# Attention and a hidden layer on one core: masks built in steps, exp(h) kept in PSUM, a low-bit step on ScalarE, the range check last

## The chip, the cores and the metric

The kernel runs on one core of a Trainium2 chip. A core has a matrix engine (TensorE, PE in the profile), three engines for elementwise work (VectorE = DVE, ScalarE = ACT, GpSimd = POOL) and SyncE (SP), which here issues the DMA transfers. Each engine takes its own instructions in order and waits on semaphores for the others. The metric is the device time of one execution in microseconds (us); smaller is better.

## The reference

The input holds 4 sequences of 768 tokens and 8 heads of 64. Each token attends to itself and the 127 before it, and to the first `n_sink` = 4 tokens of its sequence. The result goes through a layer of 2048 hidden units with an ELU.

```python
scores = scale * np.matmul(q, k.transpose(0, 1, 3, 2))
keep = is_sink | in_window
scores = np.where(keep, scores, -1000000000.0)
...
a = a / (np.sum(a, axis=-1, keepdims=True) + 1e-09)
return np.matmul(a, v).astype(np.float32)
...
h = x @ w_in
g = np.where(h > 0.0, h, alpha * (np.exp(np.minimum(h, 0.0)) - 1.0))
return (g @ w_out).astype(np.float32)
```

Here x is the attention's result, 3072 tokens of 512. The hidden layer's weights (512 x 2048 and 2048 x 512) arrive as float64; q, k and v are float32.

## The kernel before

**Precision.** Products are made of 16-bit halves. An operand is split into a rounded high half (by ScalarE) and the rest (by VectorE or GpSimd), and TensorE adds three products: high·high, high·low, low·high.

**Chunks.** The 24 tiles of 128 tokens are cut into nine chunks (`SIZES`): three of two tiles (256 tokens), then six of three (384). For each chunk, attention gives `x` (four pairs of heads), then the hidden layer runs over 16 groups `f` of 128 hidden units. The first two chunks are done in halves (`PARTS`): groups 0 to 7 of chunk 0, the same of chunk 1, then groups 8 to 15 of both.

**Weights** (`weights`, `weight_f32`). 32 pieces of 128 x 512, two for each group (the even piece is of `w_in`, the odd one of `w_out`), are loaded once, in the first part of the run (the ramp), in which the attention of the first chunks runs as well. A piece is 128 x 1024 words of float64 halves in `raw`. Four steps make a float32 of it: ScalarE scales the upper words into a PSUM bank, `acc[2]` (L267); VectorE shifts out the three bits that the lower word adds (L268, 16-bit integers) and takes the sign bit (L269), both into `wu`; VectorE joins the three (L270). Then ScalarE makes the high half (L416) and GpSimd the low one (L417). There are two buffers `wu` and six `raw`.

**Attention.** TensorE makes scores (L540, L541; L547 in the first two chunks), VectorE adds the mask and takes the row's minimum of the negative in one instruction (L566), ScalarE takes exp and its sum (L568), then the probabilities are split (L580 on ScalarE, L581 on VectorE) and a DMA transposes them from `pq` to `pt` (L599). TensorE multiplies with V into the single bank `po` (L610), and ScalarE and VectorE copy it out as the two halves of `x` (L623, L624); the next pair needs `po` after that.

**Hidden layer.** TensorE adds 12 products into a bank of `h` (L651). ScalarE takes exp into `g` in SBUF (L659), VectorE makes `(e - 1) * scale` in place (L661) and joins it with `h` (L662), ScalarE and GpSimd split it (L664, L665), and two groups later TensorE adds it to the chunk's output banks `acc` (L672). At the end ScalarE and VectorE copy `acc` out (L695, L697), and SP stores it.

**Masks.** `make_masks` makes three masks from `n_sink` and `window`: `m0` for a sequence's first tile, `m1` for its second, `m2` for the others. `attention_moe` first reads the two integers, makes floats of them (L940 to L945) and checks their range (L948 to L952).

**Range check.** The fast path is valid for bounded values. `in_range` (L723) reduces the sums collected on the way on VectorE, a tiny matmul (L741) spreads the verdict over the partitions, and `decide` (L733) writes the flag, which each engine reads at the end to branch past `general_path`.

**Order.** The order on every engine comes from `Plan`: each step is a task with an engine, an estimated length and dependencies. TensorE's order is written down by positions (`pos`); the others are listed by a greedy schedule with due times from TensorE's. So an estimate changes the order on ScalarE, VectorE, GpSimd and SP.

Of the kernel before, what the change touches and what calls it, by code (L numbers as in the profile page):

```python
# [280 lines left out]
def make_masks(nc, tmp, sk, nw, m0, m1, m2):  # L281
# [13 lines left out]


    nc.vector.tensor_scalar(own, rel, nw[:, 1:2], None, ALU.is_lt)
    nc.vector.tensor_scalar(kp, rel, 0.0, None, ALU.is_ge)
    nc.vector.tensor_tensor(own, own, kp, ALU.mult)

    nc.vector.tensor_copy(kp, own)
# [11 lines left out]
    nc.gpsimd.memset(m1[:, 0:NS], MASKED)

    def rest():
        to_mask(m2[:, KW + NS : 2 * KW], own)
        nc.vector.tensor_copy(kp[:, 0:NS], rel[:, 0:NS])
        to_mask(m2[:, NS:KW], kp)
        to_mask(m2[:, 0:NS], sk)

    return rest


def fast_path(tc, ctx, first, kq, vx, wt, out, nw, flag):
# [672 lines left out]
```

## Time and profile before

| | |
|---|---|
| median of 3 runs | 664.21 us (663.05 to 664.29) |
| the profiled execution | 662.14 us, its span 660.3 us |
| mean granted clock of TensorE | 0.984 |
| busy: TensorE, its weight loads | 609.9 us, 370.2 us |
| busy: VectorE, ScalarE, GpSimd | 458.4 us, 456.9 us, 338.2 us |
| transfers | 93.41 MB, 141 GB/s on average |

The span runs from the first to the last instruction; the execution's time has 1.84 us around it. The busy tenths of the page show three parts, 16.5 us to a digit:

```
PE   3486799789999999999999999999999999999996
DVE  6999998896677776667677776758677787524222
ACT  4999786777788887767677777766677777523221
```

TensorE reaches nine tenths after about a quarter of the span and keeps it to the last slice. How to read the rows that follow: a row of a group has the line, engine, operation, output and inputs with their shapes, the count, busy us and mean ns, then the idle time in front and who ended it. A row of a timeline starts with the start and length in us.

### The profile page before, as it was taken

The numbers are of one execution on the slowest core, as the hardware profiler recorded it, in microseconds if no ns is written. First come the engines' busy times: TensorE is split into PE (matmuls) and PEld (weight loads), VectorE is DVE, ScalarE is ACT, GpSimd is POOL, SyncE is SP. The second block draws the span as 40 slices with busy tenths as digits, with TensorE's granted clock in tenths as the row PEclk, the third lists the DMA queues.
The fourth block names the chain that finished last, engine by engine and source line by source line (L and its number), as shares of the span: only waits on it lengthen the run. The fifth ranks groups of instructions, "written<-read, shape, count | busy, mean of one in ns | idle before, by whom it ended". The sixth has DMA issues, their size and how long they took to land.

```text
span 660.3 us, 13443 instructions
## 1 busy us (share of the span) xinstructions
PE 609.9 (92%) x4449; PEld 370.2 (56%) x4449; DVE 458.4 (69%) x1251; ACT 456.9 (69%) x1340; POOL 338.2 (51%) x497
## 2 busy tenths in 40 slices
PE   3486799789999999999999999999999999999996
PEld 2343466456776665555555556555555565555552
DVE  6999998896677776667677776758677787524222
ACT  4999786777788887767677777766677777523221
POOL 0158866785556666544555655444446564322221
PEclk9999698899999999999999999999999999999998
DMA  7989974857654586435454566555554734211001
GB/s 264 206 282 266 276 199 144 269 142 167 145 118 128 136 184 131 116 92 171 116 152 118 133 156 167 104 111 171 112 155 128 208 84 101 49 56 49 1 0 54
DMA packets 130110, 93.41 MB, mean 141 GB/s; under 512 B 104432, under 2 KB 109552, under 8 KB 130032
## 3 DMA queue, kind: packets, MB, share of 16 engines
q1 hardware_dynamic: 130032, 92.47, 53.2%
q8 instruction: 37, 0.61, 0.4%
q14 instruction: 41, 0.34, 0.2%
HBM read 59.94 MB, written 7.34 MB: 102 GB/s over the span
## 4 chain that ended last, share of the span: by engine, by line
PE 78%; DVE 7%; ACT 5%; issue 4%; POOL 3%; DMA 3%; SPq 0%; DVEq 0%; POOLq 0%; ACTq 0%
PE h L651 33%; PE acc L672 33%; PE po L610 5%; PE s L540 3%; PE s L541 3%; DMA pt<-pq 2%; PE s L547 1%; ACT e L568 1%; DVE wu L268 1%; POOL kq L487 1%; DVE wv L270 1%; DVE wu L269 1%; DVE pq L581 1%; DVE g L661 1%; POOL kq L489 1%
## 5 line engine op out<-in xcount | busy, mean ns | idle before, releaser
L651 PE MATMUL h<-x,w 128*128 128x384 f16 (+1 forms) x1728 | 276.6, 310 | 5.6 <-DVE g L662 5.6
L665 POOL TENSOR_TENSOR gl<-g,gh 128x384 f16<-128x384 f32 (+1 forms) x144 | 126.9, 882 | 215.2 <-ACT gh L664 184.4
L651 PEld LDWEIGHTS <-w 128*128 128x128 f16 x1728 | 165.6, 99 | 98.7 <-issue 5.9
L672 PE MATMUL acc<-w,gh 128*128 128x512 f16 x768 | 195.3, 384 | 0.8 <-DVE wv L693 0.8
L661 DVE TENSOR_SCALAR g<-g 128x384 f32<-128x384 f32 (+1 forms) x144 | 65.3, 454 | 115.8 <-ACT g L659 115.3
L659 ACT ACTIVATE g<-h 128x384 f32<-128x384 f32 (+1 forms) x144 | 64.9, 451 | 88.3 <-PE h L651 83.1
L581 DVE SCALAR_TENSOR_TENSOR pq<-e,st,pq 128x256 f16<-128x256 f32 (+1 forms) x192 | 107.2, 587 | 19.7 <-ACT pq L580 19.1
L672 PE MATMUL acc<-w,gl 128*128 128x512 f16 x384 | 110.6, 383 | 0.6 <-POOL gl L665 0.4
L672 PEld LDWEIGHTS <-gh 128*128 128x128 f16 x768 | 70.9, 98 | 71.5 <-issue 3.0
L568 ACT ACTIVATE e<-e,st 128x264 f32<-128x264 f32 (+1 forms) x192 | 93.4, 487 | 11.1 <-DVE st L566 9.7
L664 ACT ACTIVATE gh<-g 128x384 f16<-128x384 f32 (+1 forms) x144 | 69.3, 481 | 44.6 <-DVE g L662 44.2
L566 DVE CUSTOM_DVE_ANT_0 e<-s,m 128x264 f32<-128x264 f32 (+1 forms) x192 | 73.0, 404 | 32.1 <-PE s L541 26.8
L580 ACT ACTIVATE pq<-e,st 128x256 f16<-128x256 f32 (+1 forms) x192 | 85.1, 480 | 10.5 <-DVE st L573 10.1
L487 POOL TENSOR_TENSOR kq<-kqs,kq 128x396 fp32r<-128x396 f32 (+1 forms) x56 | 67.2, 1199 | 23.9 <-ACT kq L483 23.0
L662 DVE SCALAR_TENSOR_TENSOR g<-g,h 128x384 f32<-128x384 f32 (+1 forms) x144 | 72.6, 504 | 1.6
L672 PEld LDWEIGHTS <-gl 128*128 128x128 f16 x384 | 37.6, 99 | 47.9 <-POOL gl L665 2.5
L483 ACT ACTIVATE kq<-kqs 128x780 fp32r<-128x780 f32 (+2 forms) x56 | 48.4, 879 | 17.1 <-PE s L541 14.3
L417 POOL TENSOR_TENSOR w<-wv,w 128x512 f16<-128x512 f32 x32 | 39.5, 1236 | 38.8 <-ACT w L416 18.9
L489 POOL TENSOR_TENSOR kq<-kqs,kq 64x384 fp32r<-64x384 f32 (+1 forms) x56 | 56.7, 1013 | 4.4
L610 PE MATMUL po<-pt,vh 128*64 128x128 f16 x704 | 41.7, 230 | 17.8 <-DMA pt<-pq 7.8
L540 PE MATMUL s<-kq 128*128 128x264 f32 x160 | 56.2, 370 | 1.7 <-POOL kq L489 1.6
L610 PEld LDWEIGHTS <-vh 128*64 128x64 f16 x704 | 31.1, 115 | 29.6 <-issue 21.7
(78 smaller groups left out, 629.2 us busy)
## 6 DMA issues: line engine op xcount, KB each, us to landing
raw<-in_wt_dram SPq DMA_DIRECT2D x32, 512.0 KB, 5.6
kqs<-in_kq_dram SPq DMA_DIRECT2D x24, 456.0 KB, 3.4
kqs<-in_kq_dram SPq DMA_DIRECT2D x24, 390.0 KB, 3.3
out_dram<-wv SPq DMA_DIRECT2D x24, 256.0 KB, 2.5
vs<-in_vx_dram SPq DMA_DIRECT2D x20, 256.0 KB, 3.1
vm<-in_vx_dram SPq DMA_DIRECT2D x6, 768.0 KB, 4.6
kqs<-in_kq_dram SPq DMA_DIRECT2D x12, 326.0 KB, 4.1
vs<-in_vx_dram SPq DMA_DIRECT2D x12, 320.0 KB, 3.1
```

Of the source, the lines that this page charges most:

```text
L487: nc.gpsimd.tensor_tensor(buf[:, KQ_MAX : KQ_MAX + n] if c >= DUP else buf[:, kw : 2 * kw], raw[:, :n], hi[:, :n].bitcast(F32), ALU.subtract)
L540: nc.tensor.matmul(sp[:, :wd], q, hi[:, c0 : c0 + wd], start=True, stop=False)
L566: red = add("DVE", 0.13 + 0.00145 * wd, lambda ee=ee, me=me, sp=sps[e], m=m, wd=wd: nc.vector.tensor_tensor_reduce(ee, sp[:, :wd], m[:, :w ...
L568: ex = add("ACT", 0.48 + 0.00085 * wd, lambda ee=ee, me=me, rs=rs[:, e : e + 1]: nc.scalar.activation(ee, ee, AF.Exp, bias=me, scale=-1.0, ...
L580: a = add("ACT", act_us(nb * P, True), lambda src=src, hi=hi, re=re: nc.scalar.activation(hi, src, AF.Copy, scale=re), deps=[rr])
L581: b = add("DVE", dve_us(nb * P) + 0.1, lambda src=src, hi=hi, lo=lo, re=re: nc.vector.scalar_tensor_tensor(lo, src, re, hi, ALU.mult, ALU. ...
L610: nc.tensor.matmul(po[e * D : (e + 1) * D, oc], vv[:, vo : vo + D], pt[:, (2 * e + part) * nb + i, :], start=new, stop=last)
L651: nc.tensor.matmul(hp[:, :n], win[:, part, d, :], xx[:, :n], start=k == 0, stop=k == 3 * ND - 1)
L661: b = add("DVE", 0.1 + 0.0008 * n, lambda gf=gf: nc.vector.tensor_scalar(gf, gf, -1.0, G_SCALE, ALU.add, ALU.mult), deps=[a])
L662: b = add("DVE", dve_us(n), lambda gf=gf, hp=hp: nc.vector.scalar_tensor_tensor(gf, gf, 0.0, hp[:, :n], ALU.min, ALU.max), deps=[b])
L665: tl = add("POOL", pool_us(n), lambda gl=gl, gf=gf, gh=gh: nc.gpsimd.tensor_tensor(gl[:, :n], gf, gh[:, :n], ALU.subtract), deps=[th])
L672: nc.tensor.matmul(acc[i], gg[:, i * P : (i + 1) * P], wout[:, part, :], start=f == f0 and k == 0, stop=f == f1 - 1 and k == 2)
```

## The change

Four edits, and the planner's estimates with them.

1. The masks are made by a generator in four steps. Before the integers are there: what needs only the row numbers, and the constant columns (GpSimd). Then `m0`, then `m1`, then `m2`; the last two are tasks of the plan, on which the first reductions of a second and a third tile depend. `m0` and `m1` write the four sink columns again in place of a copy. The range check of the integers (`allowed`) becomes a task of its own, wanted by the last check only.
2. Where exp(h) fits beside h in its PSUM bank (256 tokens: chunks 0 to 2), ScalarE writes it there and L661's successor (L673) reads it from there.
3. For every even piece of weights (`ON_ACT`) the shift by 13 bits is an activation of ScalarE (L276): multiply by 2^-13, add a little less than -1/2, round to a 16-bit integer.
4. The range check waits for the last group's `g`, and its matmul stands behind all others.

```diff
+ON_ACT = range(0, NW, 2)
...
+    if on_act:
+        steps[1] = lambda: nc.scalar.activation(ui[:, :, 0], halves[:, :, 1], AF.Copy, scale=2.0**-13, bias=-4095.5 / 8192)
+    return steps
...
+    nc.vector.tensor_scalar(kp, rel, 0.0, None, ALU.is_ge)
...
+    yield
+
+    nc.vector.tensor_scalar(sk, sk, nw[:, 0:1], None, ALU.is_lt)
+    nc.vector.scalar_tensor_tensor(own, rel, nw[:, 1:2], kp, ALU.is_lt, ALU.mult)
+    to_mask(m0[:, NS:KW], own)
+    nc.vector.tensor_tensor(kp[:, 0:NS], own[:, 0:NS], sk, ALU.max)
+    to_mask(m0[:, NS : 2 * NS], kp[:, 0:NS])
+    yield
     to_mask(m1[:, KW + NS : 2 * KW], own)
     nc.vector.tensor_scalar(kp, rel, float(P), nw[:, 1:2], ALU.add, ALU.is_lt)
-    nc.vector.tensor_copy(rel[:, 0:NS], kp[:, 0:NS])
-    nc.vector.tensor_tensor(kp[:, 0:NS], kp[:, 0:NS], sk, ALU.max)
     to_mask(m1[:, NS:KW], kp)
+    nc.vector.tensor_tensor(rel[:, 0:NS], kp[:, 0:NS], sk, ALU.max)
+    to_mask(m1[:, NS : 2 * NS], rel[:, 0:NS])
+    yield
+    to_mask(m2[:, KW + NS : 2 * KW], own)
+    to_mask(m2[:, NS:KW], kp)
+    to_mask(m2[:, 0:NS], sk)
+    yield
...
-    rest_ = add("DVE", 0.9, rest)
+    mask1 = add("DVE", 1.0, lambda: next(masks))
+    mask2 = add("DVE", 0.6, lambda: next(masks), deps=[mask1])
+    allowed = add("DVE", 0.7, allowed)
...
-            u1 = add("DVE", 0.65, step(1), deps=[ld])
+            u1 = add("ACT", act_us(512), step(1), deps=[ld]) if k in ON_ACT else add("DVE", 0.65, step(1), deps=[ld])
...
-        tl = add("POOL", 1.5, ...
+        tl = add("POOL", 1.22, ...
...
-            a = add("ACT", act_us(n) + 0.06, lambda gf=gf, hp=hp, sums=sums: nc.scalar.activation(gf, hp[:, :n], AF.Exp, scale=1.0 / G_SCALE, accum_out=sums), deps=[s1])
+            ex = hp[:, n : 2 * n] if 2 * n <= 512 else gf
+            a = add("ACT", act_us(n) + 0.15, lambda ex=ex, hp=hp, sums=sums: nc.scalar.activation(ex, hp[:, :n], AF.Exp, scale=1.0 / G_SCALE, accum_out=sums), deps=[s1])
-            b = add("DVE", 0.1 + 0.0008 * n, lambda gf=gf: nc.vector.tensor_scalar(gf, gf, -1.0, G_SCALE, ALU.add, ALU.mult), deps=[a])
+            b = add("DVE", 0.4 if 2 * n <= 512 else 0.45, lambda gf=gf, ex=ex: nc.vector.tensor_scalar(gf, ex, -1.0, G_SCALE, ALU.add, ALU.mult), deps=[a])
...
-    a = add("DVE", 2.0, in_range, deps=seen + exps_done)
-    b = add("PE", 0.1, lambda: nc.tensor.matmul(sp[:, 0:3], ones, some16, start=True, stop=True), deps=[a], pos=start + 2 * LAG - 1.5)
+    a = add("DVE", 2.0, in_range, deps=seen + exps_done + g_done[-1:] + [allowed])
+    b = add("PE", 0.1, lambda: nc.tensor.matmul(sp[:, 0:3], ones, some16, start=True, stop=True), deps=[a], pos=start + 2 * LAG)
```

Three places of the order show what moves. First VectorE's, near its beginning. Before the change, the last rows ahead of the first reduction of scores (L566); the range check of the integers (L948 to L951) and five more rows stand ahead of these.

```order
L294 TENSOR_SCALAR m1_173<-pt5_108 128x128
L294 TENSOR_SCALAR m2_174<-pt5_108 128x128
L302 TENSOR_TENSOR pt5_108<-pt5_108 128x4
L294 TENSOR_SCALAR m0_172<-pt5_108 128x128
L309 TENSOR_SCALAR pt5_108<-pt5_108,words_58 128x128
L310 COPY pt5_108<-pt5_108 128x4
L311 TENSOR_TENSOR pt5_108<-pt5_108 128x4
L294 TENSOR_SCALAR m1_173<-pt5_108 128x128
L317 COPY pt5_108<-pt5_108 128x4
L294 TENSOR_SCALAR m2_174<-pt5_108 128x128
L294 TENSOR_SCALAR m2_174<-pt5_108 128x4
L566 ISA e0_91,st0_94<-s0_166,m0_172 128x132
```

In the changed kernel all that stands there behind the integers' conversion:

```order
L307 TENSOR_SCALAR pt5_99<-pt5_99,words_58 128x4
L309 SCALAR_TENSOR_TENSOR pt5_99<-pt5_99,words_58 128x128
L303 TENSOR_SCALAR m0_163<-pt5_99 128x128
L312 TENSOR_TENSOR pt5_99<-pt5_99 128x4
L303 TENSOR_SCALAR m1_164<-pt5_99 128x128
L303 TENSOR_SCALAR m0_163<-pt5_99 128x4
L317 TENSOR_SCALAR pt5_99<-pt5_99,words_58 128x128
L303 TENSOR_SCALAR m1_164<-pt5_99 128x128
L319 TENSOR_TENSOR pt5_99<-pt5_99 128x4
L303 TENSOR_SCALAR m1_164<-pt5_99 128x4
L576 ISA e0_82,st0_85<-s0_157,m0_163 128x132
L576 ISA st0_85 128x1
```

Of 20 instructions behind the conversion ten are left ahead of the first reduction; the writes of `m2` stand behind the two reductions of the first tile, the integers' range check 28 rows behind the first of them.

Second, ScalarE's order where chunk 0's attention ends: the second to the fourth copy of `x` out of `po`, with the weight steps between (`acc2` is the scaled upper words, `w` a finished high half). Before:

```order
L623 ACTIVATE x_117<-po0_168 128x256
L510 ACTIVATE vh1_87<-vs1_73 128x384
L267 ACTIVATE acc2_171<-raw2_128 128x512
L416 ACTIVATE w1_133<-wv1_121 128x512
L623 ACTIVATE x_117<-po0_168 128x256
L510 ACTIVATE vh0_86<-vs0_72 128x512
L267 ACTIVATE acc2_171<-raw3_129 128x512
L416 ACTIVATE w2_134<-wv2_122 128x512
L267 ACTIVATE acc2_171<-raw4_130 128x512
L416 ACTIVATE w3_135<-wv3_123 128x512
L623 ACTIVATE x_117<-po0_168 128x256
```

And after the change:

```order
L633 ACTIVATE x_108<-po0_159 128x256
L520 ACTIVATE vh1_78<-vs1_64 128x384
L426 ACTIVATE w0_123<-wv0_111 128x512
L270 ACTIVATE acc2_162<-raw2_119 128x512
L633 ACTIVATE x_108<-po0_159 128x256
L276 ACTIVATE wu0_115<-raw2_119 128x512
L426 ACTIVATE w1_124<-wv1_112 128x512
L270 ACTIVATE acc2_162<-raw3_120 128x512
L426 ACTIVATE w2_125<-wv2_113 128x512
L633 ACTIVATE x_108<-po0_159 128x256
L270 ACTIVATE acc2_162<-raw4_121 128x512
L276 ACTIVATE wu0_115<-raw4_121 128x512
```

The copies keep their rows; two rows that make low bits (`wu0`) stand behind the third and the fourth copy, and each finished weight comes one piece later.

Third, VectorE's order at the end of the run: `g` of the last group, the check (`checks`, `some`), the flag in `words`, and the last copies out of `acc`. Before:

```order
L727 TENSOR_REDUCE some_203<-checks_202 128x1 x2
L728 TENSOR_SCALAR checks_202<-checks_202 128x32
L729 TENSOR_REDUCE some_203<-checks_202 128x1
L730 TENSOR_SCALAR some_203<-some_203 128x2
L731 CAST some16_204<-some_203 128x3
L662 SCALAR_TENSOR_TENSOR g1_110<-g1_110,h1_165 128x384
L735 TENSOR_REDUCE some_203<-s0_166 128x1
L736 TENSOR_SCALAR some_203<-some_203 128x1
L737 TENSOR_TENSOR words_58<-words_58,some_203 128x1
L967 CAST words_58<-words_58 128x1
L697 TENSOR_SCALAR wv1_121<-acc0_169 128x512
L697 TENSOR_SCALAR wv3_123<-acc2_171 128x512
```

And after the change:

```order
L674 SCALAR_TENSOR_TENSOR g1_101<-g1_101,h1_156 128x384
L738 TENSOR_SCALAR checks_191<-checks_191 128x144
L738 TENSOR_SCALAR checks_191<-checks_191 128x36
L740 TENSOR_REDUCE some_192<-checks_191 128x1 x2
L741 TENSOR_SCALAR checks_191<-checks_191 128x32
L742 TENSOR_REDUCE some_192<-checks_191 128x1
L743 TENSOR_SCALAR some_192<-some_192 128x2
L744 CAST some16_193<-some_192 128x3
L710 TENSOR_SCALAR wv1_112<-acc0_160 128x512
L710 TENSOR_SCALAR wv3_114<-acc2_162 128x512
L748 TENSOR_REDUCE some_192<-s0_157 128x1
L749 TENSOR_SCALAR some_192<-some_192 128x1
```

The check now stands behind the last group's `g` and its verdict behind the copies out of `acc`.

More of the change, by code (lines that the diff above doesn't have):

```diff
@@ L265, in weight_f32 @@
     halves = raw.bitcast(U16).rearrange("p (f t) -> p f t", t=4)
-    return (
+    steps = [
         lambda: nc.scalar.activation(d, words[:, :, 1].bitcast(F32), AF.Copy, scale=2.0**-111),
@@ L287, in make_masks, with fast_path @@
     nc.vector.tensor_copy(rel, ri)
+    nc.vector.tensor_scalar(kp, rel, 0.0, None, ALU.is_ge)
     for j in range(NS):
         nc.gpsimd.memset(sk[:, j : j + 1], float(j))
-    nc.vector.tensor_scalar(sk, sk, nw[:, 0:1], None, ALU.is_lt)
+    for m in (m0, m1):
+        nc.gpsimd.memset(m[:, 0:NS], MASKED)
+    for m in (m1, m2):
+        nc.gpsimd.memset(m[:, KW : KW + NS], MASKED)
     def to_mask(dst, keep):
         nc.vector.tensor_scalar(dst, keep, -1.0, -MASKED, ALU.add, ALU.mult)
[L297 to L301, printed above, removed]
-    nc.vector.tensor_tensor(kp[:, 0:NS], kp[:, 0:NS], sk, ALU.max)
-    to_mask(m0[:, NS:KW], kp)
-    nc.gpsimd.memset(m0[:, 0:NS], MASKED)
+    yield
[5 more added lines that the diff above has]
+    yield
     to_mask(m1[:, KW + NS : 2 * KW], own)
-    for m in (m1, m2):
-        nc.gpsimd.memset(m[:, KW : KW + NS], MASKED)
     nc.vector.tensor_scalar(kp, rel, float(P), nw[:, 1:2], ALU.add, ALU.is_lt)
-    nc.vector.tensor_copy(rel[:, 0:NS], kp[:, 0:NS])
-    nc.vector.tensor_tensor(kp[:, 0:NS], kp[:, 0:NS], sk, ALU.max)
     to_mask(m1[:, NS:KW], kp)
[L313 to L324, printed above, removed]
+    nc.vector.tensor_tensor(rel[:, 0:NS], kp[:, 0:NS], sk, ALU.max)
[5 more added lines that the diff above has]
+    yield
+def fast_path(tc, ctx, first, kq, vx, wt, out, nw, flag, scalars, allowed):
     nc = tc.nc
@@ L362, in fast_path @@
     tmp = pts[-1].rearrange("p b k -> p (b k)").bitcast(F32)
-    rest = make_masks(nc, tmp[:, : 4 * P], tmp[:, 4 * P : 4 * P + NS], nw, m0, m1, m2)
+    masks = make_masks(nc, tmp[:, : 4 * P], tmp[:, 4 * P : 4 * P + NS], nw, m0, m1, m2)
+    next(masks)
+    scalars()
+    next(masks)
     nc.gpsimd.memset(ones, 1.0)
@@ L399, in step @@
         def step(i):
-            return lambda: weight_f32(nc, v, acc[2], wu[k % RINGS["wu"]], raw)[i]()
+            return lambda: weight_f32(nc, v, acc[2], wu[k % RINGS["wu"]], raw, k in ON_ACT)[i]()
         ld = add("SP", 0.4, load, deps=[w_done.get(k - AHEAD, [None])[0]], lat=dma_us(P * 512 * 8))
@@ L701, in feed_forward @@
             evacs[i] = ev
-    saved, exps_done = {}, []
+    saved, exps_done, g_done = {}, [], []
     start = 0
@@ L964, in attention_moe @@
         with ExitStack() as inner:
-            fast_path(tc, inner, first, kq, vx, wt, out, nw, f[:, 0:1])
+            fast_path(tc, inner, first, kq, vx, wt, out, nw, f[:, 0:1], scalars, allowed)
         nc.vector.tensor_copy(flag, f[:, 0:1])
```

33 lines of the change are left out of this document (18 added, 15 removed).

## The prediction, made before the changed kernel had run

> **What bounds the kernel now.** I read the busy times of the page first, then the same by stages, then what TensorE waited for, then single instructions.
>
> ```profile
> PE 609.9 (92%) x4449; PEld 370.2 (56%) x4449; DVE 458.4 (69%) x1251; ACT 456.9 (69%) x1340; POOL 338.2 (51%) x497
> ```
>
> TensorE is busy for 92% of the span, so about 50 us of the 660.3 can be won at all. The stages say where. The columns are the stretch, its length, busy time of TensorE, its weight loads, VectorE, ScalarE and GpSimd, the granted clock, the DMA share and rate.
>
> ```profile
> core 0: us, PE busy (x) PEld busy (x) DVE busy (x) ACT busy (x) POOL busy (x), PEclk, DMA share, GB/s
> 6.33:20.00 13.67, 6.75 (x24) 4.03 (x24) 12.23 (x60) 10.24 (x37) 1.16 (x1) 1.00 0.93 329
> 20.00:40.00 20.00, 13.18 (x118) 8.93 (x116) 19.14 (x61) 17.95 (x56) 5.22 (x7) 1.00 0.96 269
> 40.00:60.00 20.00, 15.48 (x136) 9.44 (x135) 19.28 (x56) 19.61 (x62) 13.52 (x22) 1.00 0.97 271
> 60.00:80.00 20.00, 12.30 (x92) 7.99 (x90) 20.00 (x42) 15.04 (x40) 16.54 (x23) 0.74 0.92 241
> 80.00:100.00 20.00, 17.88 (x144) 12.51 (x144) 18.74 (x43) 17.85 (x53) 14.69 (x20) 1.00 0.78 216
> ...
> 120.00:140.00 20.00, 15.95 (x116) 9.87 (x115) 17.28 (x37) 15.57 (x42) 15.35 (x16) 0.91 0.65 208
> ...
> 240.00:400.00 160.00, 160.00 (x1143) 94.21 (x1141) 110.40 (x305) 118.47 (x341) 87.58 (x128) 1.00 0.53 134
> ```
>
> From 240 to 400 us, and by the same view on to 640, TensorE has no gap (160.00 of 160.00): nothing done to the other engines helps there. From 6.33 to 80 us it is busy for 47.7 of 73.7 us, and VectorE for 70.7 (12.23 + 19.14 + 19.28 + 20.00), so VectorE sets the pace. ScalarE comes close behind with 62.8 and is full from 40 to 60 us (19.61 of 20). The DMA share is above 0.9, too. TensorE's own waits name the same engine:
>
> ```profile
> PE s L547 <- DVE st L566: 10.7, 10, 2.7
> PE po L610 <- DMA pt<-pq: 7.8, 6, 2.5
> PE po L610 <- DVE x L624: 7.7, 3, 4.1
> ...
> PE h L651 <- DVE g L662: 5.6, 5, 2.3
> ```
>
> Of the four rows 24.0 us end on VectorE (10.7 + 7.7 + 5.6), against 7.8 us on the transposes of the probabilities. The two steps which the change takes from VectorE or makes free of stretching are in the next view, grouped by form over 6.3 to 230 us; the number behind the count is the busy time, then the mean in ns.
>
> ```profile
> L661 DVE TENSOR_SCALAR g<-g 128x256 f32<-128x256 f32 x48 | 23.8, 497 | 12.8 <-ACT g L659 12.6
> L269 DVE TENSOR_SCALAR wu<-raw 128x512 uint16<-128x512 uint16 x32 | 22.6, 707 | 2.8 <-DMA raw<-in_wt_dram 2.7
> L270 DVE SCALAR_TENSOR_TENSOR wv<-acc,wu 128x512 int32<-128x512 int32 x32 | 21.7, 679 | 0.7 <-ACT w L416 0.4 <-ACT acc L267 0.2
> L268 DVE TENSOR_SCALAR wu<-raw 128x512 uint16<-128x512 uint16 x32 | 20.9, 654 | 0.0
> L267 ACT ACTIVATE acc<-raw 128x512 f32<-128x512 f32 x32 | 20.2, 630 | 2.2 <-DVE wv L270 1.3 <-DMA raw<-in_wt_dram 0.7
> ...
> L662 DVE SCALAR_TENSOR_TENSOR g<-g,h 128x256 f32<-128x256 f32 x48 | 19.8, 412 | 0.5
> L664 ACT ACTIVATE gh<-g 128x256 f16<-128x256 f32 x48 | 19.6, 409 | 10.6 <-DVE g L662 10.5
> ...
> L483 ACT ACTIVATE kq<-kqs 128x912 fp32r<-128x912 f32 x4 | 3.8, 960 | 0.6 <-PE s L541 0.6
> ```
>
> The means hide two populations. Instructions of VectorE whose operands all lie in SBUF stretch at times; those with a PSUM operand (L270 and L662) keep to their length:
>
> ```profile
> 53.72 0.28 DVE L661 TENSOR_SCALAR g<-g 128x256 f32<-128x256 f32 x1
> 66.56 1.12 DVE L661 TENSOR_SCALAR g<-g 128x256 f32<-128x256 f32 x1
> 68.89 1.40 DVE L268 TENSOR_SCALAR wu<-raw 128x512 uint16<-128x512 uint16 x1
> ```
>
> L661 takes 0.28 us or 1.12, L268 up to 1.40. GpSimd, the last of the busy columns above, works 16.54 of the 20 us there, so I take the excess for waiting on GpSimd's use of SBUF.
>
> **The change part by part.** The sums are made against the profiled execution, 662.14 us with a span of 660.3.
>
> *Masks in steps, range check of the scalars later.*
>
> ```profile
> 6.25 0.15 DVE L948 TENSOR_SCALAR words<-words 128x1 f32<-128x1 f32 x1
> ...
> 9.53 0.29 DVE L566 CUSTOM_DVE_ANT_0 e<-s,m 128x132 f32<-128x132 f32 x1
> ...
> 9.88 1.46 PE L547 MATMUL s<-kqs 64*128 64x264 f32 x4 [2.74 <-DVE st L566]
> ```
>
> Between 6.25 us and the first score's reduction at 9.53 VectorE runs 20 instructions (3.28 us, 0.164 each); TensorE waits 2.74 us for that reduction. The new order has 10 there, so 10 × 0.164 = **1.6 us** are freed. Three mask writes follow the reductions and five small instructions stand later (first place of the order above): they are still executed and return up to 0.5 us, which leaves **−1.1**. What covers it afterwards is VectorE's queue itself: it is full until 80 us, so this is part of the sum there and not added twice.
>
> *Three low bits by ScalarE.* 16 of the 32 L268 leave VectorE: 16 × 0.654 = 10.5 us, and 16 activations over 512 elements join ScalarE. No row has an activation with 16-bit integers on both sides. The nearest is L267, which reads the same words and has the same width (0.630); bounds are the shortest and the longest row of ScalarE quoted, 0.409 at half the width (L664) and 0.960 at 912 (L483). I take 0.63, 10.1 us in all. The change also adds a wait: L273 of an even piece now needs this activation. In the second place of the order L276 for raw2 stands behind the copy of x; L273 waits for it with the next weight steps and the low half of the last x of the chunk queued behind, and TensorE's po bank waits for that. L267 was already waited for there, so a meeting costs what is left of 0.63 after VectorE's low half of x, some 0.4 as L662: 0.2 us. SP's order moves with it: the load of the sixth piece now stands behind eight transposes and not three. Five pieces lie ahead of it in SBUF, which hides that; without that cover L272 would wait as long as the transposes are issued.
>
> *Exp in PSUM.* For the chunks of 256 tokens (48 of 144 groups) L661 has its input in PSUM. Nearest is L662, one operand there, same width: 0.412. So 48 × (0.497 − 0.412) = 4.1 us less; bounded by 0 and by 48 × (0.497 − 0.28) = 10.4. Where nothing stretched it now, each is 0.13 longer, hidden as the result is wanted two groups later.
>
> [...]
>
> *The sum until 80 us.* Take the eighth low half of x, the end of chunk 1's attention:
>
> ```profile
> 82.86 0.40 DVE L624 SCALAR_TENSOR_TENSOR x<-po,x 128x256 f16<-128x256 f32 x1
> ```
>
> Counted in both orders, 16 finished weight pieces and 8 groups of the hidden layer stand ahead of it in either. The low-bit step stands there 9 times in place of 17, the sign step 18 in place of 17: −8 × 0.654 + 0.707 = −4.5. Masks −1.1, L661 −8 × 0.085 = −0.7: VectorE has **−6.3** ahead. ScalarE has 8 activations more, and one weight step, one split of V, one of keys and one of g less: 8 × 0.63 − 4 × 0.63 = +2.5. Its idle time from 6.33 to 80 us is 73.7 − 62.8 = 10.9, of which up to 3.2 lie ahead of the first reduction at 9.53. Losing 6.3 of length and 2.5 to work leaves 2.1: less than it idles at the start. Both engines in order and both full is not to be had, so I take about two thirds, **−4.0**.
>
> *From 80 to 230 us* 8 low-bit steps (5.2 us) and 40 L661 (3.4 us) lighten VectorE further, but TensorE is 80 to 90% busy and its long waits are for transposes, which the change does not shorten. I take **−1.0** for waits on g.
>
> *The tail.*
>
> ```profile
> 645.02 0.36 DVE L661 TENSOR_SCALAR g<-g 128x384 f32<-128x384 f32 x1 [2.94 <-ACT g L659]
> 645.42 0.56 DVE L662 SCALAR_TENSOR_TENSOR g<-g,h 128x384 f32<-128x384 f32 x1
> ...
> 648.92 0.36 DVE L661 TENSOR_SCALAR g<-g 128x384 f32<-128x384 f32 x1 [2.94 <-ACT g L659]
> ...
> 650.47 0.55 DVE L662 SCALAR_TENSOR_TENSOR g<-g,h 128x384 f32<-128x384 f32 x1
> ...
> 651.71 0.91 POOL L665 TENSOR_TENSOR gl<-g,gh 128x384 f16<-128x384 f32 x1 [4.13 <-issue]
> ...
> 652.16 0.16 DVE L735 TENSOR_REDUCE some<-s 128x1 f32<-128x3 f32 x1 [1.14 <-PE s L741]
> ...
> 652.67 0.10 PEld L672 LDWEIGHTS <-gl 128*128 128x128 f16 x1 [0.62 <-POOL gl L665]
> 652.74 0.15 DVE L967 CAST words<-words 128x1 int32<-128x1 f32 x1
> ...
> 654.40 0.69 DVE L697 TENSOR_SCALAR wv<-acc 128x512 f32<-128x512 f32 x1 [0.60 <-PE acc L672]
> ```
>
> Normally L662 follows L661's start by 0.40 us; for the last group eight instructions of the range check stand between and it is 1.55. g is 1.15 us late, GpSimd's low half with it, and TensorE waits 0.62 for it. The new order has the check behind (third place of the order): the 0.62 goes. What is late next is the verdict: its matmul is now TensorE's last, its three small steps (L735 and on) and L967's successor stand behind the last copy L697. That copy ends at 655.09 − 0.62 = 654.47, and the four steps take 652.74 + 0.15 − 652.16 = 0.73, so the flag is there at 655.2 instead of 652.9. Until now SP came last, whose issue of the last store follows 655.09. Bounds −0.6 and +0.2, I take **−0.3**.
>
> Sum: −4.0 − 1.0 − 0.3 = −5.3, that is 656.8 against 662.14. The median of the runs, 664.21, lies 2.07 above the profiled one; I keep that and predict 664.2 − 5.3 = **658.9 us**.
>
> **Rivals.**
>
> *ScalarE becomes the bound.* It has 0.39 us idle between 40 and 60 us and 2.05 in the 20 before. Eight new activations stand ahead of the eighth x. The copies of x wait behind them in ScalarE's queue and TensorE's po bank for the copies; where ScalarE comes to a copy later than VectorE to its half, each costs its whole length, 8 × 0.63 = 5.0, and VectorE's relief is idle time. It decides from the point at which ScalarE's new work exceeds those 2.4 us of idle, four activations. Less masks, L661 and tail (1.1 + 0.7 + 0.3) that is +2.9: 667.1, slower. An activation at the upper bound of 0.960 would end here. Against it: until 80 us ScalarE has 7.9 us less work than VectorE now, and only 2.5 are added. Chance 0.13.
>
> *The transposes set the pace.* The DMA share is 0.92 to 0.97 until 80 us. If packets are the limit, a faster VectorE only waits for them; half the start and the tail remain, −0.9: 663.3. Against it: TensorE's waits name them for 7.8 us only. Chance 0.12.
>
> *The ramp follows VectorE wholly.* −6.3 until 80 us, −2.9 for its waits on g behind, −0.6: −9.8. There is a clock effect as well:
>
> ```profile
> 66.69 0.42 PE L610 MATMUL po<-pt,vh 128*64 128x128 f16 x4 [4.08 <-DVE x L624]
> ```
>
> ```profile
> 70.64 2.72 PE h L651 x12
> ...
> 103.90 1.34 PE h L651 x12
> ```
>
> After a gap of 4.08 us TensorE takes 2.72 us for a group that takes 1.34 at other times, and the stage's granted clock is 0.74. If the gap shrinks, 1.4 us come back: 653.0 in all. [...] Chance 0.15.
>
> That the change does nothing measurable, since the new orders undo what is saved, is part of the second rival.
>
> **How the numbers follow.** Forecast 0.60 at 658.9, rivals 0.13, 0.12 and 0.15. The range is 653.0 to 664.0: it leaves out the first rival and half of the third. A measurement tells some 0.2% (1.3 us) from no change. Faster by more: 0.60 + 0.15 + a third of the second, 0.79; within: 0.08; slower: 0.13.
>
> **What would show it.** In the new profile the first reduction starts near 8.4 us; VectorE's busy time is 12 to 16 us less, ScalarE's 8 to 12 more; the activation with integers shows about 0.63; L661's successor at 256 shows one length near 0.41; TensorE's waits for VectorE in 0 to 230 us fall from 24 to under 20; the last group's L662 follows by 0.4. It is wrong if TensorE's waits are only renamed, from VectorE to ScalarE or the transposes, with the eighth x no earlier than 81 us.

## The result, and the profile after

| | us |
|---|---|
| kernel before, median of 4 runs | 663.63 (661.84 to 664.29) |
| changed kernel, median of 4 runs | 673.52 (669.53 to 674.60) |
| ratio | 1.0137, 95% interval 1.0097 to 1.0176 |
| profiled execution of the changed kernel, its span | 669.53, 667.7 |
| predicted | 658.9 (653.0 to 664.0) |

The change makes the kernel slower by 1.4%. The ratio is taken from the single runs, six of the changed kernel in all, and is not the quotient of the two medians. The profiled execution is the fastest of its kernel, so the traces show 7.4 us of the loss (spans of 660.3 and 667.7) and not all of it. Of the changed kernel, the lines that answer to those shown of before: L671 is exp(h), L673 and L674 make g, L677 and L678 split it, L661 and L685 are TensorE's products, L620 and L634 those of `po` and its copy, L609 the transposes, L405 the loads of weights, L270 to L273 and L276 the weight steps. The page's busy times first:

```profile
PE 610.9 (91%) x4449; PEld 370.8 (56%) x4449; DVE 445.5 (67%) x1233; ACT 467.8 (70%) x1356; POOL 334.7 (50%) x497
```

VectorE has lost 12.9 us of work, ScalarE has gained 10.9, both as forecast. Then the groups by form, over 6.3 to 230 us (count, busy us, mean ns, idle time in front and who ended it):

```profile
L276 ACT ACTIVATE wu<-raw 128x512 uint16<-128x512 uint16 x16 | 12.3, 772 | 1.1 <-DMA raw<-in_wt_dram 1.1
...
L272 DVE TENSOR_SCALAR wu<-raw 128x512 uint16<-128x512 uint16 x32 | 20.2, 630 | 7.2 <-DMA raw<-in_wt_dram 7.0
L673 DVE TENSOR_SCALAR g<-h 128x256 f32<-128x256 f32 x48 | 20.1, 418 | 18.1 <-ACT h L671 14.2 <-POOL kq L497 2.0 <-POOL st L597 1.0
```

L673 has the forecast length (0.418 us). VectorE's sign step now idles 7.0 us for loads, where L269 idled 2.7. What TensorE waits for between 0 and 230 us:

```profile
PE s L557 <- DVE st L576: 8.4, 10, 1.8
...
PE h L661 <- DVE g L674: 7.2, 6, 2.3
PE po L620 <- DMA pt<-pq: 4.8, 3, 3.1
PE h L661 <- ACT h L671: 3.3, 1, 3.3
PE po L620 <- ACT pq L590: 2.6, 1, 2.6
...
PE po L620 <- DVE x L634: 1.9, 2, 1.2
PE po L620 <- ACT h L671: 1.9, 1, 1.9
PE acc L685 <- ACT gh L677: 1.8, 1, 1.8
PE po L625 <- ACT vh L526: 1.4, 1, 1.4
...
PE po L620 <- ACT wu L276: 1.2, 1, 1.2
PE h L661 <- ACT w L426: 1.0, 1, 1.0
```

The waits for VectorE fell from 24.0 to 17.5 us (8.4 + 7.2 + 1.9), but the seven rows of ScalarE make 13.2, where before had one of 2.3: waits are renamed. The eighth low half of x, the mark of the forecast, comes later than before, not earlier (82.86 then):

```profile
85.28 0.43 DVE L634 SCALAR_TENSOR_TENSOR x<-po,x 128x256 f16<-128x256 f32 x1 [1.46 <-ACT x L633]
```

Where the time goes is read from the stages; behind the stretch and its length stand the busy times of TensorE, its weight loads, VectorE, ScalarE and GpSimd; the last three numbers are granted clock, DMA share and GB/s. Before:

```profile
0.00:60.00 60.00, 35.41 (x274) 22.41 (x275) 52.18 (x181) 49.07 (x153) 21.32 (x47) 1.00 0.89 264
60.00:160.00 100.00, 81.70 (x611) 54.59 (x609) 87.67 (x196) 76.77 (x216) 73.78 (x97) 0.91 0.72 197
160.00:240.00 80.00, 78.53 (x677) 54.23 (x676) 58.31 (x175) 65.72 (x212) 48.00 (x73) 1.00 0.60 145
240.00:640.00 400.00, 400.00 (x2822) 232.27 (x2820) 254.38 (x682) 261.38 (x751) 192.39 (x280) 1.00 0.45 113
```

After:

```profile
0.00:60.00 60.00, 35.90 (x270) 22.67 (x271) 47.68 (x169) 49.40 (x148) 19.34 (x42) 1.00 0.86 259
60.00:160.00 100.00, 78.58 (x588) 52.13 (x588) 76.92 (x180) 82.97 (x225) 70.28 (x97) 0.91 0.71 195
160.00:240.00 80.00, 77.44 (x642) 53.93 (x641) 55.30 (x176) 65.57 (x210) 49.27 (x71) 1.00 0.58 138
240.00:640.00 400.00, 398.95 (x2849) 231.94 (x2847) 257.97 (x689) 264.31 (x762) 191.22 (x282) 1.00 0.46 116
```

Up to 60 us TensorE is ahead. From 60 to 160 us it falls back by 3.1 us, although VectorE is now busy for 76.9 of the 100 us in place of 87.7: no engine is full over the whole stretch, and TensorE waits all the same. By 640 us 4.8 us are lost; its total busy time is 1.0 higher, and 1.7 are lost behind its last work (5.9 before, 7.7 after). That is the 7.4 us between the spans, to rounding.

### The profile page after: what moved, and what is told of

It is laid out like the page before. It is cut to its first block, busy times and chain, and to the rows that moved or that the text cites. A ratio compares the mean times of both kernels' runs of the same rounds, so it can differ in the third digit from the quotient of the medians.

```text
span 667.7 us, 13461 instructions
## 1 busy us (share of the span) xinstructions
PE 610.9 (91%) x4449; PEld 370.8 (56%) x4449; DVE 445.5 (67%) x1233; ACT 467.8 (70%) x1356; POOL 334.7 (50%) x497
## 4 chain that ended last, share of the span: by engine, by line
PE 75%; POOL 6%; ACT 5%; DMA 5%; DVE 4%; issue 3%; SPq 1%; POOLq 0%; DVEq 0%; ACTq 0%
PE acc L685 33%; PE h L661 32%; PE po L620 4%; PE s L550 3%; DMA pt<-pq 2%; PE s L551 2%; DMA raw<-in_wt_dram 2%; POOL kq L497 2%; POOL kq L499 1%; ACT e L578 1%; ACT pq L590 1%; DVE wv L273 1%; ACT kq L493 1%; POOL gl L678 1%; DVE wu L272 1%
## 5 line engine op out<-in xcount | busy, mean ns | idle before, releaser
L661 PE MATMUL h<-x,w 128*128 128x384 f16 (+1 forms) x1728 | 278.8, 312 | 12.9 <-DVE g L674 7.2
L678 POOL TENSOR_TENSOR gl<-g,gh 128x384 f16<-128x384 f32 (+1 forms) x144 | 125.3, 871 | 209.3 <-ACT gh L677 168.4
L661 PEld LDWEIGHTS <-w 128*128 128x128 f16 x1728 | 166.3, 99 | 106.7 <-issue 5.8
L685 PE MATMUL acc<-w,gh 128*128 128x512 f16 x768 | 194.3, 382 | 1.8 <-ACT gh L677 1.8
L685 PEld LDWEIGHTS <-gh 128*128 128x128 f16 x768 | 70.8, 98 | 72.2 <-ACT gh L677 2.3
L673 DVE TENSOR_SCALAR g<-g 128x384 f32<-128x384 f32 x96 | 42.8, 446 | 101.4 <-ACT g L671 100.9
L685 PE MATMUL acc<-w,gl 128*128 128x512 f16 x384 | 109.6, 380 | 0.4 <-POOL gl L678 0.3
L671 ACT ACTIVATE g<-h 128x384 f32<-128x384 f32 x96 | 47.1, 490 | 75.3 <-PE h L661 72.7
L677 ACT ACTIVATE gh<-g 128x384 f16<-128x384 f32 (+1 forms) x144 | 69.4, 482 | 40.3 <-DVE g L674 38.3
L674 DVE SCALAR_TENSOR_TENSOR g<-g,h 128x384 f32<-128x384 f32 (+1 forms) x144 | 72.6, 504 | 1.6
L685 PEld LDWEIGHTS <-gl 128*128 128x128 f16 x384 | 37.6, 98 | 46.9 <-POOL gl L678 1.9
L620 PE MATMUL po<-pt,vh 128*64 128x128 f16 x704 | 42.0, 231 | 13.7 <-DMA pt<-pq 5.9
L620 PEld LDWEIGHTS <-vh 128*64 128x64 f16 x704 | 31.2, 115 | 25.8 <-issue 19.0
```

The source lines that it names most:

```text
L620: nc.tensor.matmul(po[e * D : (e + 1) * D, oc], vv[:, vo : vo + D], pt[:, (2 * e + part) * nb + i, :], start=new, stop=last)
L661: nc.tensor.matmul(hp[:, :n], win[:, part, d, :], xx[:, :n], start=k == 0, stop=k == 3 * ND - 1)
L674: b = add("DVE", dve_us(n), lambda gf=gf, hp=hp: nc.vector.scalar_tensor_tensor(gf, gf, 0.0, hp[:, :n], ALU.min, ALU.max), deps=[b])
L677: th = add("ACT", act_us(n), lambda gf=gf, gh=gh: nc.scalar.activation(gh[:, :n], gf, AF.Copy), deps=[b])
L678: tl = add("POOL", pool_us(n), lambda gl=gl, gf=gf, gh=gh: nc.gpsimd.tensor_tensor(gl[:, :n], gf, gh[:, :n], ALU.subtract), deps=[th])
L685: nc.tensor.matmul(acc[i], gg[:, i * P : (i + 1) * P], wout[:, part, :], start=f == f0 and k == 0, stop=f == f1 - 1 and k == 2)
```

## The experiments

Ratios are against runs of the kernel before on the same chip. They come from the single runs and differ from the quotient of the medians by up to 0.2%. Of each edit only the lines that decide are shown.

### Which edit loses? (four runs)

Two theories: ScalarE's new step is the loss (A), or the sixth load is, which now comes late. The first run takes the step back to VectorE; the second adds the step alone to the kernel before; the third executes it on ScalarE but plans it on VectorE; the fourth lets a sixth load run ahead.

```diff
-ON_ACT = range(0, NW, 2)
+ON_ACT = range(0)
```

> The changed kernel with no low-bit step on ScalarE (all 32 stay on VectorE); masks, exp in PSUM, late check and the new estimates stay. If the ScalarE step is the loss (theory A: its 12.3 us, or the orders that it brings), this run falls to the time before or below it, 657 to 664 us. If the loss lies in the other edits or their estimates (theory B), it stays at 670 to 674.

Measured: 673.27, ratio 1.0188 (1.0124 to 1.0253).

```diff
+            u1 = add("ACT", act_us(512), step(1), deps=[ld]) if k in ON_ACT else add("DVE", 0.65, step(1), deps=[ld])
```

> The kernel before with the low-bit step of every even piece on ScalarE as its only change, planned there. Theory A: slower than before by 6 to 12 us. Theory B: within 2 us of before.

Measured: 670.82, 1.0131 (1.0077 to 1.0186).

```diff
-            u1 = add("ACT", act_us(512), step(1), deps=[ld]) if k in ON_ACT else add("DVE", 0.65, step(1), deps=[ld])
+            u1 = add("DVE", 0.65, step(1), deps=[ld])
```

> The changed kernel, the low-bit step executed by ScalarE but planned as before on VectorE, so that the order on TensorE, GpSimd and SP is that of the run without the ScalarE step. If ScalarE's added work alone costs the time (A1), it is as slow as the changed kernel, 670 to 675. If the reordering costs it, above all the sixth weight load behind eight transposes in place of three (A2), it falls to 660 to 666.

Measured: 674.81, 1.0192 (1.0133 to 1.0252).

```diff
-AHEAD = 5
+AHEAD = 6
```

> The changed kernel with six weight pieces loaded ahead in place of five. If late weight loads are the cause (A2: VectorE waited 7.0 us for raw and ScalarE 3.8), those waits fall under 4 us together and the time by 4 to 8 us, to 664 to 669. If ScalarE's work is the cause (A1), within 2 us of the changed kernel.

Measured: 670.38, 1.0138 (1.0079 to 1.0197).

Without the step the loss is the same, and with the step alone it is the same; the two don't add. A falls. With six loads ahead, VectorE and ScalarE wait 6.4 us for loads of weights in place of 10.8 (under 4 had been expected), and the ratio stays, so the late load is not the loss by itself either. What the four have in common is that each was planned anew. Their waits sit in different places: without the step TensorE waits 12.2 us for transposes, 7.6 for GpSimd's halves of weights and 1.3 for ScalarE between 0 and 230 us. So a new theory, L: the edits save what they save, but each makes the planner list the tasks in another order, and the orders lose. Its rival, W: the edits' own work costs.

### The order alone, and the edits without a new order (four runs)

First the kernel before with the change's estimates and no other edit; second, one estimate moved by 0.01.

```diff
-        tl = add("POOL", 1.5, ...
+        tl = add("POOL", 1.22, ...
-            a = add("ACT", act_us(n) + 0.06, ...
+            a = add("ACT", act_us(n) + 0.15, ...
-            b = add("DVE", 0.1 + 0.0008 * n, ...
+            b = add("DVE", 0.4 if 2 * n <= 512 else 0.45, ...
```

> The kernel before with no instruction changed, only the planner's estimates of the change (GpSimd's low half of a weight 1.5 -> 1.22, exp(h) +0.06 -> +0.15, (e - 1) * scale -> 0.40 or 0.45). 345 rows of ScalarE, 298 of VectorE, 67 of GpSimd and 48 of SP stand elsewhere than before; TensorE's order is the same. Theory L (the loss is the new order; the edits' own work saves): 667 to 674 us. Rival W (the edits' own work costs; order matters little): within 2 us of the kernel before, 660 to 666.

Measured: 671.77, 1.0115 (1.0074 to 1.0157).

```diff
-        tl = add("POOL", 1.5, ...
+        tl = add("POOL", 1.49, ...
```

> The kernel before with one estimate moved by 0.01 (GpSimd's low half of a weight 1.5 -> 1.49). 23 rows of ScalarE, 7 of VectorE, 4 of GpSimd, 2 of SP stand elsewhere. Theory L: few rows move, so within 3 us of the kernel before, either way. Theory C (the order of before is a rare lucky one, any disturbance loses most of the 9 us): 667 or more. Rival W: no difference beyond 1 us.

Measured: 662.64, 0.9989 (0.9966 to 1.0012). Few rows moved, and nothing is lost.

Third, the changed work (masks, exp(h), check) under the old tasks and estimates, so that the order stays. Fourth, ScalarE's step as well, at VectorE's places in that order:

```diff
+            ex = hp[:, n : 2 * n] if 2 * n <= 512 else gf
-            a = add("ACT", act_us(n) + 0.06, lambda gf=gf, ...
+            a = add("ACT", act_us(n) + 0.06, lambda ex=ex, ...
-    b = add("PE", 0.1, ..., deps=[a], pos=start + 2 * LAG - 1.5)
+    b = add("PE", 0.1, ..., deps=[a], pos=start + 2 * LAG)
```

> The order of before, with three of the four edits executed in it: masks in fewer steps, exp(h) in PSUM for 256 tokens, the range check behind the last g and its matmul last. All estimates and tasks are those of before, the three low bits stay on VectorE. Theory L: below the kernel before, 656 to 661 us (masks -1.1, exp in PSUM -1 to -3, against +1 to +1.5 if the late verdict costs what the tail of the changed kernel shows). Rival W: 668 or more.

Measured: 659.55, 0.9931 (0.9909 to 0.9952).

```diff
-            return lambda: weight_f32(nc, v, acc[2], wu[k % RINGS["wu"]], raw)[i]()
+            return lambda: weight_f32(nc, v, acc[2], wu[k % RINGS["wu"]], raw, k in ON_ACT)[i]()
```

> As the run of the three edits in the old order, and ScalarE makes the three low bits of the even pieces as well, at the very places where VectorE had them in the order of before. All of the change's work in the order of before, therefore. Theory L: 655 to 664, no more than 2 us from the run without the low-bit step. Rival W: 669 or more. Rival S (a step on ScalarE at VectorE's place waits in a queue that is not planned for it, as the changed kernel with such a plan showed): 666 to 672, while the run without it is below the kernel before.

Measured: 661.24, 0.9959 (0.9939 to 0.9980).

This is the deciding pair. The page of the fourth run has the same number of instructions on each engine as the changed kernel's, and busy times close to it:

```profile
PE 611.2 (92%) x4449; PEld 370.5 (56%) x4449; DVE 449.8 (68%) x1233; ACT 466.7 (71%) x1356; POOL 335.8 (51%) x497
```

The same work in the old order is faster than the kernel before, and in the planner's new order slower: 1.0137 / 0.9959 = 1.0179, **11.9 us for the order alone** (about ±3 from the two intervals). And the kernel before, with its own work in an order from new estimates, loses 1.15%. W falls; for these two orders L is shown. The stages of the run with all edits in the old order show the place:

```profile
60.00:160.00 100.00, 82.72 (x615) 54.73 (x615) 81.34 (x190) 84.16 (x230) 73.03 (x100) 0.91 0.67 199
160.00:240.00 80.00, 78.73 (x678) 54.19 (x676) 58.55 (x174) 65.95 (x212) 47.86 (x73) 1.00 0.64 145
240.00:640.00 400.00, 400.00 (x2822) 232.35 (x2821) 254.39 (x681) 261.41 (x750) 192.15 (x279) 1.00 0.45 113
```

TensorE is busy 82.72 us from 60 to 160 us there, against 78.58 in the changed kernel, with VectorE and ScalarE both busier. Its waits for ScalarE, 13.2 us in the changed kernel, are one row here:

```profile
PE acc L682 <- ACT gh L674: 0.5, 1, 0.5
```

So ScalarE's added work does not make those waits by itself. But the mark of the forecast hardly moves, although no order is new here. The eighth low half of x:

```profile
82.44 0.40 DVE L632 SCALAR_TENSOR_TENSOR x<-po,x 128x256 f16<-128x256 f32 x1
```

That is 0.42 us earlier than before. From 6.33 us to its eighth x VectorE is busy for 66.65 us in place of 73.51, so 6.9 us of its work are gone; but it waits 6.5 us for ScalarE (2.8 for the scaled words, 2.7 for the high half of the probabilities, 1.0 for the new low bits) where it waited 0.6. Without the low-bit step on ScalarE the traces of the three edits in the old order (the third run of this group, and two further down that move the check) have the eighth x at 80.70, 80.53 and 81.88. In these single traces the step's relief of VectorE comes to nothing, while the other edits bring the eighth x 1.0 to 2.3 us forward. The step stands here at VectorE's places in the order; whether another order without the loss would make use of it is not shown.

### Which rows of the order? (five runs)

Two runs take the order of one engine from the new estimates and all others from before (work of before throughout):

```diff
+        return self.merge({e: first if e in OLD_ORDER else second for e in self.HOP})
```

> The kernel before, its work unchanged, and of the run with the new estimates alone only SyncE's order (the issue of loads, transposes and stores; 48 rows elsewhere). TensorE, ScalarE, VectorE and GpSimd keep the order of before. Theory T (the loss sits in SyncE's queue: transposes behind loads of weights): 668 to 672, most of the 8.4 us of the run with the new estimates. Theory Q (it sits in the order of ScalarE and VectorE, or of GpSimd): within 2 us of the kernel before.

Measured: 687.13, 1.0360 (1.0330 to 1.0389).

> The same with only GpSimd's order from the new estimates (66 rows elsewhere), all others as before. If GpSimd's order is the cause (low halves of weights after those of g and of keys): 667 to 672, with TensorE waiting for GpSimd's weights. Theories T and the one of ScalarE and VectorE: within 2 us of the kernel before.

Measured: 676.35, 1.0212 (1.0181 to 1.0243).

Both theories missed: one engine's new order among the old ones is worse than all new ones together (671.77). A share of the loss can't be put down to one engine in this way.

So single rows. In the run with the new estimates alone, SyncE issues a load of V and one of weights, then two transposes (start, length of the issue):

```profile
75.14 0.33 SPq L507 DMA_DIRECT2D vs<-in_vx_dram  x1
75.51 0.43 SPq L395 DMA_DIRECT2D raw<-in_wt_dram  x1
76.27 6.00 SPq L599 DMA_TRANSPOSE pt<-pq  x2
```

The view of these two by tile gives their time from issue to landing, and TensorE's timeline what it costs:

```profile
DMA to landing us min/median/max: 5.8/6.5/7.3
```

```profile
83.58 0.42 PE L610 MATMUL po<-pt,vh 128*64 128x128 f16 x4 [4.81 <-DMA pt<-pq]
```

The next two runs move this one load: in the order of before to the place right ahead of the transposes, and in the new order behind them.

```diff
+        sp.insert(52, sp.pop(51))
```

> The kernel before with one row of SyncE's order moved: a load of 512 KB of weights goes from ahead of a load of V to behind it, right ahead of the two transposes that start at 74.97 us. If such rows are the loss (D): TensorE's wait for the transposes there grows from 1.6 to 4 us or more, and the time by 2 to 4 us, 665 to 667. If single rows of SyncE don't matter: within 1 us of the kernel before.

Measured: 663.06, 1.0000 (0.9981 to 1.0019).

```diff
+        sp.insert(55, sp.pop(53))
```

> The run with the new estimates alone (671.8 us), with the same load moved behind the two transposes. D: its wait of 4.81 us at 83.6 us shrinks to 2 or less, 667 to 669.5. Otherwise 671 to 673.

Measured: 667.73, 1.0071 (1.0045 to 1.0097).

By the medians this row is worth 4.0 of the 8.4 us that the new order costs. By the ratios it is 2.9 of 7.6 us, and the two intervals overlap; the single times don't (666.55 to 669.69, against 671.07 to 671.82), but the two runs were on different chips. In its trace (line numbers are shifted) the transposes land early, and in place of the wait of 4.81 stand two of 1.03 and 1.72:

```profile
73.79 0.33 SPq L542 DMA_DIRECT2D vs<-in_vx_dram  x1
74.94 4.40 SPq L634 DMA_TRANSPOSE pt<-pq  x2
79.39 1.05 SPq L430 DMA_DIRECT2D raw<-in_wt_dram  x2
```

```profile
DMA to landing us min/median/max: 3.4/3.5/3.5
```

```profile
80.80 0.30 PE L645 MATMUL po<-pt,vh 128*64 128x128 f16 x4 [1.72 <-DMA pt<-pq]
```

In the order of before the same row costs nothing. But the late transposes did not come about there: the load goes out 1.7 us ahead (73.29 to 74.97), the transposes land after 3.6 and 4.1 us, TensorE's wait for them stays at 1.6, and x comes at 82.86 as before. So D missed, and what late transposes would cost in that order is not shown.

The changed kernel has the same pattern near 78 us (a transpose issued at 78.50 behind loads at 77.32 and 77.90; TensorE waits 3.12 us). A run moves that transpose ahead of the two loads:

```diff
+        sp.insert(51, sp.pop(53))
```

> The changed kernel with one row of SyncE's order moved: the transpose that is issued at 78.50 us goes ahead of the two loads (256 KB of V, 512 KB of weights) issued in the 1.2 us before. If the pattern of the new estimates is at work here too (D): TensorE's wait of 3.12 us at 83.9 us shrinks to 1.5 or less, and the time from 673.5 to 668 to 671. If not: 672 to 675.

Measured: 673.08, 1.0132 (1.0072 to 1.0192).

The wait for the transpose goes, the time stays. VectorE's rows in its trace say why (L299 is the sign step, L701 and L661 are g and x):

```profile
84.55 0.45 DVE L299 TENSOR_SCALAR wu<-raw 128x512 uint16<-128x512 uint16 x1 [3.17 <-DMA raw<-in_wt_dram]
84.90 0.41 DVE L701 SCALAR_TENSOR_TENSOR g<-g,h 128x256 f32<-128x256 f32 x1
85.23 0.45 DVE L298 TENSOR_SCALAR wu<-raw 128x512 uint16<-128x512 uint16 x1
85.57 0.41 DVE L661 SCALAR_TENSOR_TENSOR x<-po,x 128x256 f16<-128x256 f32 x1
```

The weights, now later, hold the weight step at the head of VectorE's queue for 3.17 us, with g and x behind it; x comes at 85.57, where it came at 85.28. ScalarE's half of x had been done at 82.64.

### Is the order of before a rare one? (two runs)

All estimates of the kernel before, TensorE's excepted, are changed by a random share of at most 3%:

```diff
+        if eng != "PE":
+            dur *= 1.0 + 0.03 * (2.0 * self.rng.random() - 1.0)
```

> The kernel before, its work unchanged, each estimate of the planner (TensorE's excepted) changed by a random share of at most 3%. 39 to 48 rows of SyncE, 45 of GpSimd, some 190 of ScalarE and 210 of VectorE stand elsewhere. If the order of before is a rare good one (G): 667 to 674, as the runs planned anew had. If it is the estimates of the change that are bad ones (B): within 3 us of the kernel before, 661 to 666.

Measured: 669.33, 1.0089 (1.0061 to 1.0116).

> The same with other random numbers. G: 667 to 674. B: 661 to 666.

Measured: 663.44, 1.0012 (0.9988 to 1.0035).

One draw loses 6 us, the other nothing. So the order of before is a good one, though not the only one, and 3% in the estimates can cost 6 us. Two draws say no more on how rare it is. The six runs that were planned with the change's step or estimates (the changed kernel, the four of the first group, the new estimates; two of them share most of a plan) took 670 to 675 us; the second draw shows that a new plan need not. It also shows that the forecast's mark is a weak one: its eighth x starts at 85.03, 2.2 us later than in the kernel before, and its span is 659.6.

### The end (three runs)

In the changed kernel the verdict is the last thing. VectorE's rows at its end:

```profile
660.06 0.69 DVE L710 TENSOR_SCALAR wv<-acc 128x512 f32<-128x512 f32 x1 [0.60 <-PE s L754]
...
661.23 0.15 DVE L985 CAST words<-words 128x1 int32<-128x1 f32 x1
```

The flag is there at 661.38 and the span ends at 667.7, 6.3 us later; it ends 6.95 behind the last copy, where before it was 5.2 (655.09 to 660.3). Two runs move the check in the kernel with three edits in the old order: to its old place, and with its matmul behind the last chunk's first tile. A third does the latter to the changed kernel (with the moved transpose).

```diff
-    a = add("DVE", 2.0, in_range, deps=seen + exps_done + g_done[-1:])
-    b = add("PE", 0.1, ..., deps=[a], pos=start + 2 * LAG)
+    a = add("DVE", 2.0, in_range, deps=seen + exps_done)
+    b = add("PE", 0.1, ..., deps=[a], pos=start + 2 * LAG - 1.5)
```

> As the three edits in the old order, but the last range check and its matmul stand where they stood before (ahead of the last group's (e - 1) joined with h). The last copy comes 0.6 us later, as the last group's low half waits again, and the flag is ready ahead of it. If the execution ends 5.2 us behind the last copy or 6.3 behind the flag, whichever is later (the traces of before and after), this one ends 1.0 us earlier than with the check last: 658 to 659.5. If the place of the check is worth the 0.3 us that the prediction gave it: 0.3 later.

Measured: 658.07, 0.9920 (0.9896 to 0.9944), 1.5 us below the check at the end.

```diff
-    b = add("PE", 0.1, ..., deps=[a], pos=start + 2 * LAG)
+    b = add("PE", 0.1, ..., deps=[a], pos=start + 2 * LAG - 0.995)
```

> As the three edits in the old order, with the range check behind the last g, but its matmul after the products of the last chunk's first tile rather than behind all. By the rule of the run above both the flag (about 652.4 in the time of that trace) and the last copy come early: 1.0 to 1.7 us earlier than with the check last, 658 us, the best so far. If the end does not hang on the flag: no difference.

Measured: 658.35, 0.9920 (0.9896 to 0.9944), 1.2 us below.

> The same, and the matmul of the range check stands behind the products of the last chunk's first tile, not behind all. If the end of the execution hangs on the flag (6.3 us behind it, against 5.2 behind the last copy): 1.0 to 1.7 us below the run with the transpose alone, that is 667 to 670. If not: the same as that run.

Measured: 671.59, 1.0101 (1.0066 to 1.0135), 1.5 us below the run before it.

Three times 1.2 to 1.5 us by the medians (0.7, 0.7 and 2.1 by the ratios), each with overlapping intervals: likely, not proven one by one. The rule that I had put down (5.2 behind the copy or 6.3 behind the flag) doesn't hold in general: with the early check the span ended 6.3 us behind its last copy (653.13 to 659.4). All traces together say more. From TensorE's last matmul to the end of the span it is 7.6 to 7.7 us in the seven with the check last, and 5.9 to 7.2, with a median of 6.8, in the 13 others; the 5.9 is the trace of the kernel before. So the late check costs some 0.8 us there, and not the 1.7 between the two traces of the result. What the end waits for is not shown. The two runs with the early check in the old order are the fastest kernels of the study, 0.8% below before.

## Why the prediction was wrong

The step that failed is "the sum until 80 us": it counted the work that stands ahead of the eighth x in both orders (VectorE −6.3, ScalarE +2.5) and took two thirds of the relief, −4.0, as if the time to a place followed the work ahead of it. In the old order, where nothing else changes, VectorE's relief came about as counted (6.9 us) and the eighth x was 0.42 us earlier: VectorE waited 6.5 us for ScalarE in place of 0.6. The forecast had taken a meeting with ScalarE at 0.2 us. The order was read for counts and for one row of SyncE ("five pieces lie ahead of it in SBUF, which hides that"), but a new order had no price of its own. Nor was that row hidden: L272 idles 7.0 us for loads in the changed kernel and 2.2 in the old order. The runs give the order a price: 11.9 us at equal work, 8.4 (7.6 by the ratio) with the work of before. In the changed kernel VectorE has its 11 us of relief between 60 and 160 us, and TensorE loses 3.1 there.

By the other steps:

- **Masks, −1.1**: right at their place. The first reduction starts at 7.98 (forecast 8.4), and TensorE's second score at 8.34, where it was 9.88.
- **exp(h) in PSUM, −4.1 of VectorE's time**: right as a length (0.418 against 0.412; 23.8 to 20.1 us, −3.7). What the prediction took for the cause of the stretching agrees with its trace: over 256 elements the 19 L661 with no GpSimd instruction beside them take at most 0.30 us, and all 18 that take more than 0.31 (up to 1.24) have one beside them. L662 keeps to 0.40 to 0.42 either way, and so does L673 after the change.
- **Three low bits, 0.63 each on ScalarE**: mis-sized. An activation on 16-bit integers takes 0.772, 12.3 us in all. In the old order the step doesn't pay: 0.9959 with it, 0.9931 without, +1.9 us, with an uncertainty of 2.0 from the two intervals, and its trace has the eighth x later than the three without it.
- **−4.0 until 80 us and −1.0 after**: even in the old order all edits together give −0.41% (2.7 us by the ratio), not −5.3. So of the miss of 14.6 us about 12 belong to the order and the rest to VectorE's waits for ScalarE, to these sizes and to the end.
- **The tail, −0.3**: wrong sign, as far as the runs tell. The 0.62 us wait is gone and L674 follows L673 by 0.40, as forecast. But the span ends 6.95 us behind the last copy instead of 5.2, 1.7 later in these two traces and some 0.8 over all, for 0.62 gained. The prediction had ended its sum at the flag (655.2 against a copy at 654.47) and not at what follows it.
- **ScalarE becomes the bound (0.13)**: right sign, wrong mechanism; without the step the loss is the same, and with it in the old order TensorE waits 0.5 us for ScalarE.
- **"The new orders undo what is saved"**, put under the second rival: the right mechanism, but bounded at no gain. Nothing bounds it there.

What the prediction named as the sign against it is what came: the waits are renamed, and the eighth x is later than 81 us.

Open stays which rows lose in the changed kernel. One row of SyncE did about half of it (by the medians) in the order with new estimates; in the changed kernel the like repair only handed the wait to VectorE's queue.

## What to carry to other kernels

Where a planner makes the order, an edit or a new estimate is two changes: the work and a newly drawn order. Time them apart, first by running the new work in the old order, then by drawing several orders (small jitter of the estimates) and keeping the fastest. Before counting on relief of a busy engine, look at whether what stands at the head of the queues, a load or another engine's step, is there in time: here 6.9 us less work for VectorE brought the eighth x forward by 0.42 us, as VectorE then waited 6.5 us for ScalarE.

## What the hardware showed

- With the new estimates alone, two transposes, the first issued 0.76 us behind a 512 KB load, land after 5.8 and 7.3 us; with the load behind them, after 3.4 and 3.5. That is 2.4 to 3.8 us more; what delays them is not shown.
- In the changed kernel ScalarE's activation from 16-bit integers to 16-bit integers, 128 x 512 (L276), takes 0.772 us, where float32 of the same width into PSUM (L270) takes 0.624.
- TensorE's granted clock fell after waits of 3.31 and 2.35 us in the changed kernel, and not after one of 2.38 us in another run. In the changed kernel the wait of 3.31 us ends at 77.72, and by stretches of 2 us the clock is then

```profile
76.00:78.00 2.00, 0.28 (x3) 0.26 (x3) 2.00 (x6) 1.96 (x7) 1.85 (x4) 1.00 1.32 105
78.00:80.00 2.00, 2.00 (x15) 1.29 (x15) 1.46 (x4) 1.59 (x5) 2.00 (x3) 0.59 1.04 230
80.00:82.00 2.00, 0.75 (x14) 0.61 (x11) 0.91 (x2) 1.89 (x7) 2.00 (x3) 0.50 0.85 277
```

  The 12 products behind that wait take 2.15 us, where 1.47 is usual. In the same trace the wait of 2.35 us ends at 122.71, the clock is 0.50 from 122.72 to 126.10, and the 12 products behind it take 2.72. With the transpose moved, a wait of 2.38 us ends at 120.05, the 12 products take 1.47, and the clock is 1.00 over the stretch from 120 to 140 us. In the trace of before, a wait of 2.53 us ends at 123.66, and the clock is 0.50 from 124.30 to 127.00. So the wait of 2.35 us cost 1.25 us beyond itself in these products, and the 1.4 us of the prediction's third rival need not come back when its gap of 4.08 us shrinks to some 2.4. What makes the clock fall is not shown.
